# Local and global attention with a GELU feed-forward layer on one Trainium2 core: the fourth chunk's second layer in plain products, word checks from step 33, casts and penalties on ScalarE, row maxima put off, P6 first, outputs by SP

## The chip, the cores and the metric

The kernel runs on one core of a Trainium2 chip. The metric is device time in microseconds (us), the median of several executions. The engines go by their names in a profile: PE (TensorE's matrix products; PEld are its weight loads), DVE (VectorE), ACT (ScalarE), POOL (GpSimd) and SP (SyncE, which here only issues DMAs).

## The reference, cut to what matters

Attention over 4 batches, 8 heads, 768 positions and a head width of 64, with 8 global keys and a window of 96 local ones, and then a feed-forward layer on the 3072 rows of 512 that it gives:

```python
scores = scale * q @ k.T - slopes * dist        # kept where is_global | is_local, else -1e9
a = exp(scores - max(scores)); a = a / (sum(a) + 1e-09)
x = (a @ v).transpose(0, 2, 1, 3).reshape(B * S, H * D)   # 3072 x 512
h = x @ w_in                                              # 512 -> 2048
g = 0.5 * h * (1.0 + erf(h / sqrt(2)))
out = g @ w_out                                           # 2048 -> 512
```

The weights arrive as 64-bit floats and are read as pairs of 32-bit words.

## The kernel before, in words

**Chunks and steps.** The 3072 rows are cut into 12 chunks of 256 rows (c = 0 to 11), the 2048 hidden columns into 8 slices of 256 (s = 0 to 7). A step (c, s) computes one slice of both layers for one chunk. `STEPS` lists 99 places, T = 0 to 98: chunks 0 and 1 take turns up to T = 18, and from there chunk c owns the eight steps that begin at T = 19 + 8 (c - 2); so chunk 3 begins at T = 27, chunk 4 at 35, chunk 5 at 43. `run` walks over T and records, for each, the first layer of step T + 1 (`m1`, tile h), its GELU, the second layer of step T (`m2`), and pieces of the attention of a later chunk.

**Values as pairs.** Each factor is kept as two 16-bit halves, high and low, and a product is three products on PE (high by high, high by low, low by high). `m1` is 24 products of 256 columns. A plain `m2` (lines 853 to 868) is 12 products of 512 columns, into two PSUM banks `acc`. From chunk `SEVEN` = 3 on, `m2_seven` forms the second layer by Strassen's seven products P1 to P7: 21 products of 256 columns, into four banks `seven`. It needs sums of blocks on both sides: `gelu7` makes the left ones (tile ss, four DVE additions at line 742, then a cast `sh` on ACT and the low half `sl` on DVE) and `sums` the right ones, once for each slice (tiles sb, sf, sw; DVE, with one cast on ACT), at the steps that `SUMS` names.

**GELU.** ACT writes the value (gr). In the plain form DVE makes the high half (gh, line 834) and the low half (gl, line 204); in the form with sums ACT makes gh.

**Where the seven products live.** `HOME` gives each product a bank and a half of it: P1 and P2 share bank 0, P6 and P7 bank 1, P4 and P5 bank 2, and P3 has bank 3. At a chunk's last step `combine` empties them on DVE (tiles u and o, line 789) in the order bank 0, bank 1, bank 2, bank 3, while the next chunk's first step already computes. That step's products come in the order of `PARTS`: P1, P2, P4, then attention work of a later chunk, then P6, P7, P5, P3.

**Attention.** For a chunk from 3 on: score products (tile s), the subtraction of penalties with a running minimum on DVE (n, mn), exponentials on ACT, normalisation on POOL (line 554), a transposition on DVE (ptb), products with v (tile av; 256 small products and loads in a row), and the copies to x on ACT and DVE. The penalties come from `more_pens`; `scale_pens` multiplies them by each head's slope with eight POOL instructions at T = 14 and 15 (line 422).

**Checks.** Each of the 32 weight pieces is loaded a second time (tile c) and folded into a mask on DVE (`check_words`, tile wand), every second step from T = 21. `rows` takes row maxima of finished output (DVE, tile otop).

**What sets the order.** Within each engine a scheduler sorts the recorded instructions; `after`, `behind` and `turn` pin some of them. From T = 19 on PE's order is as recorded (`turn`). DMAs that one engine issues leave in its order; the outputs of the chunks with seven products are issued by ACT (line 823).

The two lines on which the order of products and the choice of form hang are:

```python
SEVEN = 3
PARTS = (("P1", "P2", "P4"), ("P6", "P7", "P5", "P3"))
```

Of the kernel before, what the change touches and what calls it, by code (L numbers as in the profile page):

```python
# [13 lines left out]
AF = mybir.ActivationFunctionType  # L14
ALU = mybir.AluOpType
# [3 lines left out]
P = 128  # L19
# [12 lines left out]
NCH = B * CPB  # L32
# [12 lines left out]
GAP = 3  # L45
# [12 lines left out]
CAT = 2  # L58
# [4 lines left out]
GS = 2.0 ** 6  # L63
# [1 line left out]
WMAX = 0.5  # L65
OMIN = 2.0 ** -10
RATIO = 16.0
SEVEN = 3
PARTS = (("P1", "P2", "P4"), ("P6", "P7", "P5", "P3"))
ENDS = (("P6", "P7", "P5"), (("P1", "P2", "P6", "P7"), ("P4", "P5", "P3")))  # L70
SUMS = {17: 0, 18: 1, 19: 2, 21: 3, 22: 4, 25: 5, 26: 6, 29: 7}
HOME = {"P1": (0, 0), "P2": (0, 1), "P6": (1, 0), "P7": (1, 1), "P4": (2, 0), "P5": (2, 1), "P3": (3, 0)}
FACTORS = {"P1": ("A11", "B11"), "P2": ("A12", "B21"), "P3": ("S4", "B22"), "P4": ("A22", "T4"), "P5": ("S1", "T1"),
           "P6": ("S2", "T2"), "P7": ("S3", "T3")}
# [2 lines left out]
NB = NW // NG  # L77
KA = NW + 2 * NG
PENS = 13


def dap(t, off, dims):
# [23 lines left out]
def slope(h):  # L106
    return 2.0 ** (-(h + 1))


class Fast:  # L110
# [225 lines left out]
            sync(vv[rows, :, 7, :], dap(self.v, b * S * DM + p * P, [[DM, NG], [2 * P, 2], [1, P]]))  # L336

    def load_v(self, c):
        if c >= SEVEN:
            return self.load_windows(c)  # L340
        self.vr[c] = self.nat.tile([P, 4, DM], F32, name=f"vr{c}", tag="vn")
        self.rows_v(self.sync_of(c, (3, 3)), self.vr[c], *divmod(c, CPB))

    def load(self, c):
        sync = self.sync_of(c, (3, 0))
        b, cc = divmod(c, CPB)
        k0 = b * H * D * S
        q0 = k0 + cc * CT
        every = [[S, P], [P * S, NP]]
        qr = self.nat.tile([P, NP, CT], F32, name=f"qr{c}", tag="qn")  # L350
        if c >= SEVEN:
            kr = self.nat.tile([P, NP, 2, 2 * KA], F32, name=f"kr{c}", tag="kn")
            sync(qr, dap(self.qT, q0, every + [[1, CT]]))
            for j in range(2):
                for a in range(2):
                    for o, n, k in self.runs(cc * CT + j * P + a * HQ - NC, NW):
                        sync(kr[:, :, j, a * KA + NG + o:a * KA + NG + o + n], dap(self.kT, k0 + k, every + [[1, n]]))
                    for o in (a * KA, a * KA + NG + NW):
                        sync(kr[:, :, j, o:o + NG], dap(self.kT, k0, every + [[1, NG]]))
            self.raw[c] = (kr, qr)  # L360
            return
        kr = self.nat.tile([P, NP, KW + 96 if cc == 0 else 2 * KW], F32, name=f"kr{c}", tag="kn",
                           padded_shape=[P, NP, 4 * KA])
        sync(qr, dap(self.qT, q0, every + [[1, CT]]))
        keys = lambda o, n, k: sync(kr[:, :, o:o + n], dap(self.kT, k, every + [[1, n]]))
        if cc == 0:
            keys(0, CT, k0)
            keys(CT, 96, k0)
            keys(CT + 96, NG, k0)
        else:  # L370
            keys(NG, NX + NC, q0 - 96)
            keys(224, NX, q0 + HQ)
            keys(KW, NX, q0 + 32)
            keys(KW + 96, NX + NC, q0 + 96)
            for o in (0, 192, KW + NX, KW + 256):
                keys(o, NG, k0)
        self.raw[c] = (kr, qr)
# [41 lines left out]
    def scale_pens(self, k):  # L419
        for i in range(4):  # L420
            h = 4 * (i // 2) + i % 2
            self.nc.gpsimd.tensor_scalar(out=self.pens2[k][:, i], in0=self.base[k], scalar1=8.0 * slope(h), scalar2=0.0,
                                         op0=ALU.mult, op1=ALU.add)

    def scores_windows(self, c, n):
        nc = self.nc
# [29 lines left out]
                self.last_dve = ins.ins  # L456

    def scores_pair(self, c, p):
        if c >= SEVEN:
            return self.scores_windows(c, p)  # L460

        nc = self.nc
# [63 lines left out]
    def exps(self, c, p):  # L526
        nc = self.nc
        first = c % CPB == 0
        mn, su = self.stat.pop((c, p))
        if c >= SEVEN:  # L530
            every = [(self.pt_n[c, p][:, i], i) for i in range(4)]
        else:
            every = [(self.pt_n[c, 2 * p + hh][:, j * NK:j * NK + (P if first and j == 0 else NK)], 2 * hh + j)
                     for hh in range(2) for j in range(2)]
        for nn, i in every:
            self.table(nc.scalar.activation(out=nn, in_=nn, func=AF.Exp, bias=mn[:, i:i + 1],  # L536
                                            scale=-1.0, accum_out=su[:, i:i + 1]))
        if c < SEVEN:
            self.norm(c, p, mn, su, every)
        else:  # L540
            self.normed[c, p] = mn, su, every

    def norm(self, c, p, mn, su, every):
        nc = self.nc
        ins = nc.vector.tensor_scalar(out=su, in0=su, scalar1=1e-9, scalar2=1.0 / XS, op0=ALU.add, op1=ALU.mult)
        if c >= SEVEN:
            self.behind(ins)
        nc.vector.reciprocal(out=su, in_=su)  # L548
        if c >= 3:
            top = self.nmax[:, 3 * NP]  # L550
            nc.vector.tensor_tensor(out=top, in0=top, in1=mn, op=ALU.max)
        for nn, i in every:
            eng = nc.vector if c < 2 else nc.gpsimd
            ins = eng.tensor_scalar(out=nn, in0=nn, scalar1=su[:, i:i + 1], scalar2=0.0,  # L554
                                    op0=ALU.mult, op1=ALU.add)
        if c < 2:
            self.last_dve = ins.ins
# [193 lines left out]
    def m2_seven(self, t, part):  # L751
# [2 lines left out]
            self.seven = [self.ps_acc.tile([P, 2, 256], F32, name=f"seven{i}", tag="ps_acc") for i in range(2)]  # L754
            self.seven += [self.bank([P, 2, 256], f"seven{i}") for i in range(2, 4)]
        back = len(STEPS) - 1 - t
        names = PARTS[part] if back > 1 or (back, part) == (1, 0) else ENDS[0] if back else ENDS[1][part]
        for name in names:
            if (back, name) == (0, "P3"):
                self.products(t - 1, name)  # L760
# [48 lines left out]
    def give(self, c, k, final):  # L809
# [10 lines left out]
        if c == NCH - 1:  # L820
            (nc.sync if k else nc.scalar).dma_start(self.out[r:r + P, 256:], o[:, 1])
            return
        nc.scalar.dma_start(self.out[r:r + P, :], o.rearrange("p h c -> p (h c)"))

    def gelu(self, t):
        nc = self.nc
# [4 lines left out]
        gl = self.gp.tile([P, 2, CT], F16, name=f"gl{t}", tag="gl")  # L831
        gr = self.gp.tile([P, 2, CT], F32, name=f"gr{t}", tag="gr")
        self.table(nc.scalar.activation(out=gr, in_=hp, func=AF.Gelu, scale=1.0 / (WS * XS)))
        nc.vector.tensor_scalar(out=gh, in0=gr, scalar1=GS, scalar2=None, op0=ALU.mult)
        self.last_dve = self.lo_dve(gl, gr, gh, GS).ins
        self.g[t] = (gh, gl)

    def m2(self, t, k):
# [12 lines left out]
                    self.send(k, kk)  # L851
            return
        if s == 0:
            if c == 1:
                self.acc[c, k] = self.bank([P, DM], f"acc{c}_{k}")
            else:
                self.acc[c, k] = self.ps_acc.tile([P, DM], F32, name=f"acc{c}_{k}", tag="ps_acc")
# [16 lines left out]
    def send(self, c, k):  # L874
# [3 lines left out]
        scale = 1.0 / (GS * WS)  # L878
        nc.scalar.activation(out=o, in_=acc, func=AF.Copy, scale=scale)
        nc.scalar.dma_start(self.out[r:r + P, :], o)  # L880
        self.rows(c, k, o)

    def rows(self, c, k, o):
        self.behind(self.nc.vector.tensor_reduce(out=self.otop[:, c, k], in_=o.rearrange("p (h c) -> p h c", h=2),
# [18 lines left out]
                         "av": self.av_pair}[what](c, p)  # L903

    def slot(self, at):
        for c in range(SEVEN, NCH):
            r = self.T - START[c]
            if 0 <= r < 8 and (r % 4, at) in SLOTS:
                what, n = SLOTS[r % 4, at]
# [13 lines left out]
    def run(self, flag_i):  # L923
# [15 lines left out]
        for self.T in range(START[0] - 1, last):  # L939
# [10 lines left out]
                    self.split_weights(s, i)  # L950
            if 0 <= T - last + 9 < 6:
                self.checks(T - last + 9)
            k = T - 16 - GAP
            if 0 <= k < 64 and k % 2 == 0:
                self.check_load(k // 2)
            words = 2 <= k < 66 and k % 2 == 0
            if words and (T < 30 or T % 4 == 1):
                self.check_words((k - 2) // 2)
            if T == PENS:
                self.more_pens()  # L960
            if PENS < T < PENS + 3:
# [30 lines left out]
            if T % 8 == 3:  # L992
                for args in self.late_rows:
                    self.rows(*args)
                self.late_rows.clear()
            if words and T >= 30 and T % 4 == 3:
                self.check_words((k - 2) // 2)

    def checks(self, k):
        nc, sm = self.nc, self.const  # L1000
# [221 lines left out]
```

## Time and profile before

| what | us |
|---|---|
| median of 3 runs | 631.32 |
| lowest and highest run | 628.44, 632.48 |
| the profiled execution's own time | 629.22 |
| its span, first to last instruction | 627.4 |
| PE busy in the span | 599.5 |
| DVE busy | 498.1 |
| ACT busy | 352.9 |
| POOL busy | 91.0 |

The profile shows one execution. Its times are counted from the first instruction; 1.8 us of the time lie around the span. A PE record's length is modelled and reaches over the start of the next product, so busy time says little there: a stretch is better read by the starts of successive products. TensorE's granted clock is full (2.4 GHz) in all the stretches named below.

### The profile page before, as it was taken

Reading aid. Unit: us, or ns where it says so; the run is one execution under the profiler, and the core shown is the slowest. Engines: PE = TensorE matmul, PEld = TensorE weight load, DVE = VectorE, ACT = ScalarE, POOL = GpSimd, SP = SyncE. Lnnn points to the kernel's source line nnn. Section 1 sums busy time; section 2 is a strip of 40 time slices with the busy share of each in tenths; the row PEclk is TensorE's granted clock in tenths of the full one; section 3 lists DMA queues with packets and bytes.
Section 4 is the critical chain, followed back from the end, with each engine's and each line's share of the span. In section 5 each row is a group of like instructions: output and inputs, shape, how many; then the busy total and the mean of one; then the engine's idle time right before and its main releaser. Section 6 shows DMA issues by size and latency. Waiting matters only on the chain.

```text
span 627.4 us, 19513 instructions
## 1 busy us (share of the span) xinstructions
PE 599.5 (96%) x7968; PEld 464.8 (74%) x7968; DVE 498.1 (79%) x1579; ACT 352.9 (56%) x855; POOL 91.0 (14%) x188
## 2 busy tenths in 40 slices
PE   8988999999999899999999899999999999999995
PEld 5665544445676678888888788888888888888884
DVE  7979999998788786876876776876876876875885
ACT  3777577755526566466466366366466466463331
POOL 1000006253033022022022021021021021010000
PEclk9988999999999999999999999999999999999998
DMA  9948925434371284184184175164275173100001
GB/s 272 270 173 255 261 97 202 121 66 146 114 192 57 86 218 137 37 218 136 37 218 137 36 186 159 46 159 129 104 169 180 44 195 93 37 1 2 36 1 40
DMA packets 111809, 79.47 MB, mean 127 GB/s; under 512 B 54752, under 2 KB 99296, under 8 KB 111712
## 3 DMA queue, kind: packets, MB, share of 16 engines
q1 hardware_dynamic: 107120, 70.80, 39.7%
q10 hardware_dynamic: 4592, 7.34, 3.3%
q8 instruction: 65, 1.06, 0.7%
q14 instruction: 32, 0.26, 0.1%
HBM read 71.83 MB, written 6.29 MB: 125 GB/s over the span
## 4 chain that ended last, share of the span: by engine, by line
PE 63%; DVE 23%; ACT 8%; issue 3%; POOL 2%; DMA 1%; DVEq 0%; ACTq 0%; POOLq 0%
PE h L702 26%; PE seven L776 22%; PE av L604 5%; ACT n L536 4%; PE s L440 4%; DVE gl L204 2%; DVE ss L742 2%; PE acc L863 2%; POOL n L554 2%; DVE wb L249 1%; DVE wb L251 1%; PE warm_ps L520 1%; DVE o L789 1%; DVE sl L204 1%; DVE u L789 1%
## 5 line engine op out<-in xcount | busy, mean ns | idle before, releaser
L702 PE MATMUL h<-x,winh 128*128 128x256 f16 x1344 | 227.7, 274 | 4.4 <-DVE x L203 2.9
L702 PE MATMUL h<-x,winl 128*128 128x256 f16 x672 | 184.3, 274 | 0.0
L702 PEld LDWEIGHTS <-winh 128*128 128x128 f16 x1344 | 130.3, 98 | 25.0 <-issue 4.0
L554 POOL TENSOR_SCALAR n<-n,su 128x160 f32<-128x160 f32 (+1 forms) x160 | 81.1, 527 | 450.0 <-DVE su L548 286.3
L737 ACT ACTIVATE gr<-h 128x512 f32<-128x512 f32 x72 | 43.0, 597 | 109.2 <-PE h L702 96.3
L742 DVE TENSOR_TENSOR ss<-gr 128x128 f32<-128x128 f32 x144 | 35.2, 285 | 64.6 <-ACT gr L737 64.6
L744 ACT ACTIVATE sh<-ss 128x512 f16<-128x512 f32 x72 | 45.4, 630 | 66.4 <-DVE ss L742 66.4
L776 PE MATMUL seven<-sw,sh 128*128 128x256 f16 x432 | 75.0, 273 | 1.3 <-issue 1.3
L702 PEld LDWEIGHTS <-winl 128*128 128x128 f16 x672 | 66.1, 98 | 9.1 <-issue 1.2
L776 PEld LDWEIGHTS <-sh 128*128 128x128 f16 x576 | 55.0, 98 | 8.3 <-issue 1.5
L536 ACT ACTIVATE n<-n,mn 128x160 f32<-128x160 f32 x144 | 59.5, 414 | 2.7 <-DVE mn L451 2.5
L776 PE MATMUL seven<-sw,sl 128*128 128x256 f16 x216 | 58.9, 273 | 1.2 <-DVE sl L204 1.1
L204 DVE SCALAR_TENSOR_TENSOR gl<-gr,gh 128x384 f16<-128x384 f32 (+1 forms) x96 | 57.1, 594 | 0.7
L204 DVE SCALAR_TENSOR_TENSOR sl<-ss,sh 128x512 f16<-128x512 f32 x72 | 49.6, 689 | 10.0 <-ACT sh L744 10.0
L776 PEld LDWEIGHTS <-gh 128*128 128x128 f16 x432 | 41.0, 98 | 11.9 <-ACT gr L737 3.8
L451 DVE CUSTOM_DVE_ANT_0 n<-s,pens 128x160 f32<-128x160 f32 x144 | 38.0, 320 | 3.8 <-PE s L440 2.5
L743 ACT ACTIVATE gh<-gr 128x384 f16<-128x384 f32 x72 | 37.6, 523 | 3.9 <-ACT gr L737 1.8
L776 PE MATMUL seven<-wouth,gh 128*128 128x256 f16 x144 | 39.4, 274 | 0.0
L776 PE MATMUL seven<-wouth,gl 128*128 128x256 f16 x144 | 39.3, 273 | 0.0
L776 PE MATMUL seven<-woutl,gh 128*128 128x256 f16 x144 | 39.3, 273 | 0.0
L604 PEld LDWEIGHTS av<-ptb,vr 32*64 32x64 f32 x2304 | 31.3, 130 | 5.6 <-issue 5.3
L536 ACT ACT_TABLE_LOAD x22 | 28.2, 1283 | 12.3 <-DMA qr<-qT 6.5
(160 smaller groups left out, 1103.5 us busy)
## 6 DMA issues: line engine op xcount, KB each, us to landing
w<-w SPq DMA_DIRECT2D x32, 512.0 KB, 6.4
c<-w SPq DMA_DIRECT2D x32, 512.0 KB, 4.5
kr<-kT SPq DMA_DIRECT2D x34, 320.0 KB, 4.2
vr<-v SPq DMA_DIRECT2D x60, 112.0 KB, 2.6
qr<-qT SPq DMA_DIRECT2D x11, 512.0 KB, 4.3
out<-o ACTq DMA_DIRECT2D x22, 256.0 KB, 2.3
kr<-kT SPq DMA_DIRECT2D x84, 64.0 KB, 3.6
vr<-v SPq DMA_DIRECT2D x36, 32.0 KB, 2.7
```

Of the source, the lines that this page charges most:

```text
L204: return self.nc.vector.scalar_tensor_tensor(out=out, in0=in_, scalar=scale, in1=hi, op0=ALU.mult, op1=ALU.subtract)
L440: ins = nc.tensor.matmul(sp[hh][NG * i:NG * i + NG, u, :], lhsT=qq[hr, 2 * e + p, o:o + NG], rhs=kt[hr, 2 * e + p, j, k:k + NW], start=Tru ...
L451: ins = nc.vector.tensor_tensor_reduce(out=nn[:, 2 * hh + u], in0=sp[hh][:, u, :], in1=pens, scale=-0.125, scalar=3e38, op0=ALU.add, op1=A ...
L536: self.table(nc.scalar.activation(out=nn, in_=nn, func=AF.Exp, bias=mn[:, i:i + 1], scale=-1.0, accum_out=su[:, i:i + 1]))
L554: ins = eng.tensor_scalar(out=nn, in0=nn, scalar1=su[:, i:i + 1], scalar2=0.0, op0=ALU.mult, op1=ALU.add)
L604: ins = nc.tensor.matmul(banks[i][hh * D:(hh + 1) * D, u0 * NG:u1 * NG], lhsT=vv[rows, e, b, hh * D:(hh + 1) * D], rhs=g, start=n == 0, st ...
L702: ins = nc.tensor.matmul(hp[:, f, :], lhsT=w[:, d, fs], rhs=x[:, d, e, :], start=n == 0, stop=n == 3 * NP - 1).ins
L737: self.table(nc.scalar.activation(out=gr.rearrange("p i q -> p (i q)"), in_=hp.rearrange("p f q -> p (f q)"), func=AF.Gelu, scale=1.0 / (W ...
L742: self.last_sum = nc.vector.tensor_tensor(out=ss[:, o], in0=x, in1=y, op=op).ins
L743: nc.scalar.activation(out=gh, in_=gr[:, 1:], func=AF.Copy, scale=GS)
L744: self.last_table = nc.scalar.activation(out=sh, in_=ss, func=AF.Copy, scale=GS).ins
L776: ins = nc.tensor.matmul(out, lhsT=g, rhs=w, start=s == 0 and name in ("P1", "P4", "P6", "P3") and i == 0, stop=s >= NST - 4 and i == 2, s ...
```

## The change

Seven edits, none of which alters what is computed.

1. `SEVEN` goes from 3 to 4: chunk 3's second layer is done in plain products. Its attention keeps the form with windows, which now hangs on a constant of its own, `TURNS` = 3. The right-hand sums are made later (`SUMS`), and chunk 3's two `acc` banks come from the shared pool of banks.
2. The word checks (load, DVE instruction) move from steps 21 to 83 to steps 33 to 89.
3. In plain steps from chunk 2 on, ACT makes gh in place of DVE.
4. `scale_pens` moves from POOL to ACT.
5. The row maxima of the plain chunks after the first are put off to the next step with T % 8 == 3.
6. In a chunk's first step P6 comes third and P4 fifth (`OPENS`).
7. Outputs of the chunks with seven products are issued by SP in place of ACT.

```diff
-SEVEN = 3
+SEVEN = 4
+TURNS = 3
 PARTS = (("P1", "P2", "P4"), ("P6", "P7", "P5", "P3"))
+OPENS = (("P1", "P2", "P6"), ("P7", "P4", "P5", "P3"))
-SUMS = {17: 0, 18: 1, 19: 2, 21: 3, 22: 4, 25: 5, 26: 6, 29: 7}
+SUMS = {18: 0, 21: 1, 22: 2, 25: 3, 26: 4, 27: 5, 29: 6, 30: 7}
+WORDS = [T for T in range(33, 90) if T % 2 or T in (62, 70, 78)]
...
-            self.nc.gpsimd.tensor_scalar(out=self.pens2[k][:, i], in0=self.base[k], scalar1=8.0 * slope(h), scalar2=0.0,
-                                         op0=ALU.mult, op1=ALU.add)
+            self.nc.scalar.activation(out=self.pens2[k][:, i], in_=self.base[k], func=AF.Copy, scale=8.0 * slope(h))
...
-        names = PARTS[part] if back > 1 or (back, part) == (1, 0) else ENDS[0] if back else ENDS[1][part]
+        names = OPENS[part] if s == 0 else PARTS[part] if back > 1 or (back, part) == (1, 0) else ENDS[0] if back else ENDS[1][part]
...
-        nc.scalar.dma_start(self.out[r:r + P, :], o.rearrange("p h c -> p (h c)"))
+        nc.sync.dma_start(self.out[r:r + P, :], o.rearrange("p h c -> p (h c)"))
...
-        nc.vector.tensor_scalar(out=gh, in0=gr, scalar1=GS, scalar2=None, op0=ALU.mult)
+        if STEPS[t][0] < CAT:
+            nc.vector.tensor_scalar(out=gh, in0=gr, scalar1=GS, scalar2=None, op0=ALU.mult)
+        else:
+            self.last_table = nc.scalar.activation(out=gh, in_=gr, func=AF.Copy, scale=GS).ins
...
-            if c == 1:
+            if c % 2:
                 self.acc[c, k] = self.bank([P, DM], f"acc{c}_{k}")
...
-        self.rows(c, k, o)
+        if c:
+            self.late_rows.append((c, k, o))
+        else:
+            self.rows(c, k, o)
...
-            k = T - 16 - GAP
-            if 0 <= k < 64 and k % 2 == 0:
-                self.check_load(k // 2)
-            words = 2 <= k < 66 and k % 2 == 0
-            if words and (T < 30 or T % 4 == 1):
-                self.check_words((k - 2) // 2)
+            if T + 2 in WORDS:
+                self.check_load(WORDS.index(T + 2))
+            if T in WORDS and T % 4 == 1:
+                self.check_words(WORDS.index(T))
...
-            if words and T >= 30 and T % 4 == 3:
-                self.check_words((k - 2) // 2)
+            if T in WORDS and T % 4 > 1:
+                self.check_words(WORDS.index(T))
```

**DVE, between the low half of GELU 28 and the copies to x of chunk 4's first half.** A number in a name is its step or chunk: gl28 is the low half of step 28, av4 the products with v of chunk 4. Before:

```order
L204 SCALAR_TENSOR_TENSOR sl27_2688<-ss27_2686,sh27_2687 128x512
L884 TENSOR_REDUCE otop_141<-o2_0_2704 128x2
L884 TENSOR_REDUCE otop_141<-o2_1_2714 128x2
L278 SCALAR_TENSOR_TENSOR wand_135<-c0_3_2578,wand_135 128x512
L203 TENSOR_TENSOR sw6_1246<-sf6_2649,sw6_1246 128x1024
L742 TENSOR_TENSOR ss28_2749<-gr28_2746 128x128 x2
L742 TENSOR_TENSOR ss28_2749<-ss28_2749,gr28_2746 128x128
L742 TENSOR_TENSOR ss28_2749<-gr28_2746,ss28_2749 128x128
L204 SCALAR_TENSOR_TENSOR gl28_2748<-gr28_2746,gh28_2747 128x384
L204 SCALAR_TENSOR_TENSOR sl28_2751<-ss28_2749,sh28_2750 128x512
L203 TENSOR_TENSOR x_346<-av4_0_0_2774,x_346 128x128
```

Now (line numbers are those of the changed kernel, 2 to 8 higher):

```order
L207 SCALAR_TENSOR_TENSOR gl27_2655<-gr27_2656,gh27_2654 128x512
L724 TENSOR_TENSOR sb5_2678<-wouth5_1093,woutl5_1094 128x1024
L727 TENSOR_TENSOR sf4_2620<-sb4_2619,sf4_2620 128x256
L727 TENSOR_TENSOR sf5_2679<-sb5_2678 128x256 x2
L727 TENSOR_TENSOR sf5_2679<-sb5_2678,sf5_2679 128x256
L206 TENSOR_TENSOR sw4_989<-sf4_2620,sw4_989 128x1024
L727 TENSOR_TENSOR sf5_2679<-sb5_2678,sf5_2679 128x256
L207 SCALAR_TENSOR_TENSOR gl28_2713<-gr28_2714,gh28_2712 128x512
L206 TENSOR_TENSOR sw5_1095<-sf5_2679,sw5_1095 128x1024
L206 TENSOR_TENSOR x_346<-av4_0_0_2725,x_346 128x128
```

The left-hand sums of step 28, two row maxima and a word check are gone from ahead of x; the right-hand sums of another slice have come in before gl28.

**PE, the first step of chunk 5 (T = 43), from P2 to the products with v.** Before, with P4 (bank `seven2`) third:

```order
L776 MATMUL seven0_2761<-wouth0_327,gl43_4384 128x256
L776 LDWEIGHTS gh43_4383
L776 MATMUL seven2_2763<-sw0_329,gh43_4383 128x256
L776 LDWEIGHTS gl43_4384
L776 MATMUL seven2_2763<-sw0_329,gl43_4384 128x256
L604 MATMUL av6_0_0_4482<-ptb6_0_4354,vr6_4276 64x128 x2
```

Now, with P6 (bank `seven1`) there:

```order
L778 MATMUL seven0_3447<-wouth0_327,gl43_4217 128x256
L778 LDWEIGHTS sh43_4219
L778 MATMUL seven1_3448<-sw0_329,sh43_4219 128x256
L778 LDWEIGHTS sl43_4220
L778 MATMUL seven1_3448<-sw0_329,sl43_4220 128x256
L606 MATMUL av6_0_0_4315<-ptb6_0_4187,vr6_4109 64x128 x2
```

The third product now writes bank 1 and reads the left-hand sums sh and sl in place of gh and gl; P4 stands behind the products with v and P7.

**ACT, around the GELU of step 17.** Before:

```order
L833 ACTIVATE gr16_1670<-h16_1649 128x512
L581 COPY pt2_4_1660<-t2_5_1674 128x384
L833 ACTIVATE gr17_1714<-h17_1693 128x512
L581 COPY pt2_6_1704<-t2_6_1700 128x384
L581 COPY pt2_6_1704<-t2_7_1718 128x384
```

Now:

```order
L835 ACTIVATE gr16_1670<-h16_1649 128x512
L583 COPY pt2_4_1660<-t2_5_1674 128x384
L425 ACTIVATE pens_132<-rb_1453 128x640 x4
L425 ACTIVATE pens2_1451<-rb_1453 128x320 x4
L835 ACTIVATE gr17_1714<-h17_1693 128x512
L583 COPY pt2_6_1704<-t2_6_1700 128x384
L583 COPY pt2_6_1704<-t2_7_1718 128x384
```

The eight scalings of the penalties (pens, from tile rb) now stand ahead of gr17 and of two copies that empty PSUM banks.

## Rows read from the trace of the kernel before

**Rows 1.** Page, busy time: engine, us, share of the span, instructions.
```profile
PE 599.5 (96%) x7968; PEld 464.8 (74%) x7968; DVE 498.1 (79%) x1579; ACT 352.9 (56%) x855; POOL 91.0 (14%) x188
```

**Rows 2.** Page, the chain that ended last, shares by engine.
```profile
PE 63%; DVE 23%; ACT 8%; issue 3%; POOL 2%; DMA 1%; DVEq 0%; ACTq 0%; POOLq 0%
```

**Rows 3.** Chain in order of time: start us, us, what; from two plateaus.
```profile
176.02 2.59 PE acc L863 x12
...
570.92 2.29 PE seven L776 x21
```

**Rows 4.** Waits of PE, 140 to 260 us: us in total, times, longest us.
```profile
PE h L702 <- DVE x L203: 2.7, 2, 2.3
PE s L440 <- DVE x L203: 1.3, 1, 1.3
PE seven L776 <- DVE sl L204: 1.1, 1, 1.1
PE acc L863 <- DVE gh L834: 0.8, 1, 0.8
PE seven L776 <- DVE u L789: 0.4, 1, 0.4
PE acc L863 <- DVE gl L204: 0.2, 1, 0.2
```

**Rows 5.** Timeline of PE around 210 us: start us, us, instruction, [idle before <-releaser].
```profile
209.50 0.27 PE L776 MATMUL seven<-wouth,sl 128*128 128x256 f16 x1
212.06 0.38 PE L702 MATMUL h<-x,winh 128*128 128x256 f16 x2 [2.29 <-DVE x L203]
```

**Rows 6.** Timeline of DVE in the same stretch.
```profile
207.66 0.68 DVE L278 SCALAR_TENSOR_TENSOR wand<-c,wand 128x512 int32<-128x512 int32 x1
...
211.72 0.88 DVE L203 TENSOR_TENSOR x<-av,x 128x128 f16<-128x128 f32 x4
```

**Rows 7.** Waits of PE, whole span.
```profile
PE seven L776 <- DVE u L789: 2.5, 7, 0.4
...
PE seven L776 <- issue: 1.8, 2, 1.3
```

**Rows 8.** Timeline of PE where chunk 4 begins.
```profile
256.18 0.27 PE L776 MATMUL seven<-wouth,gl 128*128 128x256 f16 x1
256.81 0.38 PE L776 MATMUL seven<-sw,gh 128*128 128x256 f16 x2 [0.36 <-DVE u L789]
```

**Rows 9.** Timeline of DVE in the same stretch.
```profile
254.74 0.42 DVE L789 SCALAR_TENSOR_TENSOR u<-seven,u 128x256 f32<-128x256 f32 x1
255.08 0.69 DVE L204 SCALAR_TENSOR_TENSOR sl<-ss,sh 128x512 f16<-128x512 f32 x1
...
256.34 0.42 DVE L789 SCALAR_TENSOR_TENSOR u<-seven,u 128x256 f32<-128x256 f32 x1
```

**Rows 10.** Page, costliest groups: busy us, mean ns of one.
```profile
L742 DVE TENSOR_TENSOR ss<-gr 128x128 f32<-128x128 f32 x144 | 35.2, 285 | 64.6 <-ACT gr L737 64.6
L744 ACT ACTIVATE sh<-ss 128x512 f16<-128x512 f32 x72 | 45.4, 630 | 66.4 <-DVE ss L742 66.4
...
L204 DVE SCALAR_TENSOR_TENSOR sl<-ss,sh 128x512 f16<-128x512 f32 x72 | 49.6, 689 | 10.0 <-ACT sh L744 10.0
...
L743 ACT ACTIVATE gh<-gr 128x384 f16<-128x384 f32 x72 | 37.6, 523 | 3.9 <-ACT gr L737 1.8
```

**Rows 11.** Groups by line, same columns.
```profile
L727 ACT CAST sw<-sf 128x1024 f16<-128x1024 f32 x8 | 8.4, 1045 | 17.5 <-DVE sf L725 17.5
```

**Rows 12.** Timeline of ACT at step 16.
```profile
131.47 0.60 ACT L833 ACTIVATE gr<-h 128x512 f32<-128x512 f32 x1 [2.70 <-DVE gl L204]
```

**Rows 13.** Timeline of DVE at step 16.
```profile
131.39 0.66 DVE L416 TENSOR_SCALAR rb<-rb 64x960 f32<-64x960 f32 x1
```

**Rows 14.** Timeline of PE at step 16.
```profile
133.90 0.39 PE L848 MATMUL acc<-wouth,gh 128*128 128x512 f16 x1
```

**Rows 15.** Page, DMA queues: packets, MB, share of 16 engines.
```profile
q8 instruction: 65, 1.06, 0.7%
```

More of the change, by code (lines that the diff above doesn't have):

```diff
@@ L338, in load_v @@
     def load_v(self, c):
-        if c >= SEVEN:
+        if c >= TURNS:
             return self.load_windows(c)
@@ L350, in load @@
         qr = self.nat.tile([P, NP, CT], F32, name=f"qr{c}", tag="qn")
-        if c >= SEVEN:
+        if c >= TURNS:
             kr = self.nat.tile([P, NP, 2, 2 * KA], F32, name=f"kr{c}", tag="kn")
@@ L458, in scores_pair @@
     def scores_pair(self, c, p):
-        if c >= SEVEN:
+        if c >= TURNS:
             return self.scores_windows(c, p)
@@ L529, in exps @@
         mn, su = self.stat.pop((c, p))
-        if c >= SEVEN:
+        if c >= TURNS:
             every = [(self.pt_n[c, p][:, i], i) for i in range(4)]
@@ L537, in exps @@
                                             scale=-1.0, accum_out=su[:, i:i + 1]))
-        if c < SEVEN:
+        if c < TURNS:
             self.norm(c, p, mn, su, every)
@@ L545, in norm @@
         ins = nc.vector.tensor_scalar(out=su, in0=su, scalar1=1e-9, scalar2=1.0 / XS, op0=ALU.add, op1=ALU.mult)
-        if c >= SEVEN:
+        if c >= TURNS:
             self.behind(ins)
@@ L905, in slot @@
     def slot(self, at):
-        for c in range(SEVEN, NCH):
+        for c in range(TURNS, NCH):
             r = self.T - START[c]
```

## The prediction

> **What bounds the kernel now.** I read the page first. PE is busy for 96% of the span [rows 1] and carries 63% of the chain that ended last, DVE 23% [rows 2]: the reader is to see that the end is mostly PE's own work, so that two things count, the products issued and the places where PE stands still. The chain in order of time gives the price of work in stretches without a gap: a plain step's second layer takes 2.59 us (12 products of 512 columns, 0.216 each), one by seven products 2.29 us (21 of 256 columns, 0.109 each) [rows 3]. Last came PE's waits, then the timelines around the long ones. Between 140 and 260 us, chunks 2 and 3 above all, PE is let go by DVE each time [rows 4]: DVE makes the right-hand sums of all eight slices there, beside word checks and row maxima, and x comes late. From there on a wait of 0.36 us comes back where a new chunk begins, seven times with 2.5 us in all [rows 7].
>
> An idle time understates what a wait costs. The product before a gap is recorded with 0.27 us, but its successor could start after 0.11; so the gap ahead of 212.06, after a product begun at 209.50, costs 212.06 - 209.50 - 0.11 = 2.45 us where the row says 2.29 [rows 5]. I add 0.16 us to each wait.
>
> **The change part by part.**
>
> *Chunk 3 in plain products* adds on PE 8 steps x (2.59 - 2.29) = +2.4 us [rows 3], on the path, for PE has no slack there. It takes from DVE, for each of these steps, four sums of 0.285 us and one low half of 0.689 [rows 10]: 1.8 us, 14.6 us in all (the other low half grows from 384 to 512 columns, which I leave out). On its two acc banks: chunk 4 needs them some 3.6 us into its first step (24 x 0.109 of first layer, three products of 0.33), and ACT empties them in two copies, by the row for 512 columns about 0.63 each [rows 10]; no wait.
>
> *Word checks, later sums, row maxima, gh to ACT.* In the order shown, DVE loses ahead of chunk 4's first x the sums of step 28, two row maxima and a check, and gains one slice's right-hand sums, of which most stand before gl28. Before, wand began at 207.66 and x only at 211.72 [rows 6], while PE wanted it at 209.61. Seven checks leave the steps up to 33, and chunk 2's eight gh instructions leave DVE; on ACT one such cast of 512 columns takes about 0.63 us [rows 10], behind gr and ahead of gl, and ACT is busy for only 56% [rows 1]. So I let the waits of 140 to 230 us go: 2.7 + 1.3 + 1.1 + 0.8 + 0.2 = 6.1 us of idle [rows 4] (the 0.4 on u is left to the edit after this), plus six times 0.16, makes 7.1. I keep 0.3 of it, since the first right-hand sum still stands ahead of gl at the beginning of chunk 2: -6.8 us. What is late next is the sums at steps 29 and 30, in chunk 3; they have no left-hand sums beside them any more. From step 33 the checks come at the rate at which they came before (one in two steps, three more), where DVE shows no wait but the one on u.
>
> *P6 first.* At 256.18 the second product ends its issue; P4 starts at 256.81 [rows 8], because its bank is free only after DVE's third u (256.34 + 0.42). Bank 1, which P6 needs, is free after the u that begins at 254.74, and sl, P6's last factor, is written from 255.08 to 255.77 [rows 9]; P6 would start at 256.29 and want sl 0.22 later. P4 moves behind the products with v and P7. All seven waits go (six by this, that of chunk 4 by the plain chunk ahead of it): 2.5 + 7 x 0.16 = 3.6 us [rows 7]: -3.6 us.
>
> *Penalties on ACT* is the edit that can cost. The trace shows no such instruction on ACT. The nearest rows are a cast of 384 columns with 0.523 and of 512 with 0.630 us [rows 10]; a straight line gives 0.74 for 640 and 0.47 for 320 columns, for four of each 4.8 us. Bounds: four at no less than 0.63 and four at half of that, 3.8; four at the 1024-column cast's 1.045 [rows 11] and four at 0.63, 6.7. They wait for tile rb, written by 131.39 + 0.66 = 132.05 [rows 13]; gr17, which began at 131.47 [rows 12], then begins at 136.9 (135.9 to 138.8) and ends 0.6 later. Behind it wait two copies that empty banks, and on those banks PE's next scores; PE comes to them after the 12 products from 133.90 [rows 14], 133.90 + 12 x 0.216 = 136.5. So PE stands for 1.0 us (0 to 2.9). Instructions in a row overlap a little; I take +0.6. POOL loses as much work.
>
> The Trainium skill (ScalarE: Activation LUTs, What ACT_TABLE_LOAD costs) puts an ACTIVATE with immediate scale and bias at 186 ns plus 0.833 ns a column, with an overlap of 93 ns in a row; an estimate by it is 3.9 us for the eight, and PE's wait would be 0.1 us. The row for 512 columns agrees (613 ns by the rule, 630 measured).
>
> *Outputs by SP* takes from ACT a wait for DVE's last u and o. It held gr only where PE had other work, so I count nothing. On SP the two DMAs wait at most for the four microseconds in which DVE empties the banks; behind them stand the loads of a chunk that is used three steps (over 15 us) later. Cover gone: nothing up to that lead.
>
> *Sum* against the profiled execution of 629.22 us (span 627.4 and 1.8 around it): +2.4 - 6.8 - 3.6 + 0.6 = -7.4, so 621.8 us. The median of the runs, 631.32, is 2.1 above that execution; I carry the same difference over: 631.3 - 7.4 = 623.9, or 624.0 us.
>
> **The rivals.**
>
> 1. *The waits come back in another place.* The right-hand sums are as much work as before, now packed between T = 18 and 30, and x of chunk 4 still stands behind a sum's last instruction. If half of the 6.8 returns: 627.4 us. For it: the order above has sw5 directly ahead of x. Against it: DVE is rid there of 14.6 us of left-hand sums and of seven checks of 0.68 [rows 6].
> 2. *P6 first does not do what it says.* If sl or sh is late where DVE is full, P6 waits as P4 did, and 3.1 of the 3.6 us stay (six starts): 627.1. For it: sl ends only 0.7 us before it is wanted.
> 3. *Penalties dear.* With the upper bound PE stands 2.9 us in place of 0.6: 626.3.
> 4. *Instruction supply, to the slower side.* Two of PE's waits in the second product, 1.8 us, have no releaser but "issue" [rows 7], right behind the 256 dense instructions of the products with v. Queue 8 loads instructions, 65 packets of 1.06 MB [rows 15], that is 16 KB for some 245 of PE's 15,936, if all are PE's. The change takes 144 instructions from PE ahead of chunk 4, so the ends of these pieces fall elsewhere in each later pass. Seven chunks' attention, 14 passes, lies behind that place. If each stalled by the longest of these waits (1.3 + 0.16 = 1.5 us), that adds 21 us less the 2.1 that now stand: 643. It decides from about six passes on (7.4 us eaten) and is slower by over 1% from about eleven. Against it: the pieces fall at all places over the passes as it is, and two or three stall.
> 5. *No such stall at all*: the two waits vanish with the new places, 624.0 - 2.1 = 621.9.
>
> The Trainium skill (Runtime: NRT & Kernel Launch, Instruction fetch mechanics) has the sequencer load 256 instructions at a time beside execution and calls a boundary's cost mostly hidden. By it case 5 would hold in every run; the trace differs, with 1.3 us in one wait.
>
> **How the numbers follow.** The forecast has 0.47, rival 1 0.20, rival 2 0.10, rival 3 0.07, rival 4 0.08 and rival 5 0.08. About 1% of 631.3, 6.3 us, is what a measurement of this kernel can tell from no change (its three runs lie 4.0 us apart): faster means below 625.0. The forecast is only 1.0 us beyond it, so I give 0.37 of its 0.47 to faster; with rival 5 and some of rivals 1 and 3 (0.07) that makes 0.52. Slower comes from rival 4's upper part alone, 0.05 and some for what I haven't seen, 0.07. The same keeps 0.41. The range goes down to 619.0 (rival 5, with the lower bound of the penalties and 2 us of scatter) and up to 631.0 (rivals 1 and 2 together, 630.5).
>
> **What would show it.** Right: no wait of PE on x, gh or sl between 140 and 230 us; none on u at a chunk's start; chunk 3's second layer at 2.59 us a step; a wait of under 1 us on the banks at step 17; everything ahead of 130 us as before. Wrong: PE waiting for ACT at step 17 for over 2 us; waits on x or gl at steps 29 to 32; P6 waiting for sl; more "issue" waits behind the products with v.

## The result and the profile after

The changed kernel takes 621.57 us in the median of 4 runs (620.33 to 624.53), the kernel before 629.88 beside it; the ratio is 0.987 with an interval of 0.983 to 0.992. The median had been forecast at 624.0, from 631.3 for the kernel before, which came out 1.4 lower this time; the difference, 8.3 us against 7.4, is the fairer measure. The profiled execution takes 621.09 us with a span of 619.3, 8.1 us less than that of before. Page, busy time of the changed kernel and the chain that ended last:

```profile
PE 599.3 (97%) x7896; PEld 457.8 (74%) x7896; DVE 479.8 (77%) x1523; ACT 358.6 (58%) x865; POOL 81.4 (13%) x180
PE 77%; DVE 12%; ACT 4%; DMA 2%; issue 2%; SPq 2%; POOL 1%; ACTq 0%; DVEq 0%; POOLq 0%
```

Against [rows 1, 2]: PE has 72 products fewer and the same busy time, DVE's share of the chain has halved. The waits of PE from 125 us on (us in total, times, longest us):

```profile
PE acc L868 <- ACT gh L839: 1.0, 1, 1.0
PE h L704 <- DVE x L206: 0.9, 1, 0.9
PE av L606 <- issue: 0.7, 1, 0.7
PE seven L778 <- issue: 0.4, 1, 0.4
```

Of [rows 4] one wait on x and one on gh are left, the one on gh now for ACT; the seven on u of [rows 7] are gone, and "issue" has shrunk from 2.8 us in three waits (one of them on av) to 1.1 in two. Where chunk 5 begins, PE's timeline has no idle time between P2, P6 and the products with v, where [rows 8] showed P4 waiting at chunk 4's start:

```profile
300.34 0.27 PE L778 MATMUL seven<-wouth,gl 128*128 128x256 f16 x1
300.45 0.38 PE L778 MATMUL seven<-sw,sh 128*128 128x256 f16 x2
300.67 0.27 PE L778 MATMUL seven<-sw,sl 128*128 128x256 f16 x1
300.87 1.80 PE L606 MATMUL av<-ptb,vr 32*64 32x128 f32 x128
```

The starts of the same products set side by side give the account of the 8.1 us: up to step 17's first layer 0.7 later; chunk 3 in plain products +2.4 (0.30 in each of eight steps); the waits up to 230 us -5.2 (what is left of that stretch when the other terms are taken off); the seven waits on u -3.8; the waits for issue -1.8; the rest -0.4. What is left at T = 28 is seen on DVE, where x stands behind the low half of the sum recorded at T = 27:

```profile
207.93 1.23 DVE L206 TENSOR_TENSOR sw<-sf,sw 128x1024 f16<-128x1024 f32 x1 [0.51 <-ACT sw L729]
209.07 0.88 DVE L206 TENSOR_TENSOR x<-av,x 128x128 f16<-128x128 f32 x4
```

Ahead of step 19's second layer it is on ACT: the cast of the first sum stands before gr19, which had its h at about 152, and gh19 comes behind both:

```profile
152.72 1.05 ACT L729 CAST sw<-sf 128x1024 f16<-128x1024 f32 x1 [2.77 <-DVE sf L727]
...
153.67 0.59 ACT L835 ACTIVATE gr<-h 128x512 f32<-128x512 f32 x1
154.29 0.63 ACT L839 ACTIVATE gh<-gr 128x512 f16<-128x512 f32 x1
```

### The profile page after: what moved, and what is told of

It is laid out like the page before. It is cut to its first block, busy times and chain, and to the rows that moved or that the text cites. A ratio compares the mean times of both kernels' runs of the same rounds, so it can differ in the third digit from the quotient of the medians.

```text
span 619.3 us, 19315 instructions
## 1 busy us (share of the span) xinstructions
PE 599.3 (97%) x7896; PEld 457.8 (74%) x7896; DVE 479.8 (77%) x1523; ACT 358.6 (58%) x865; POOL 81.4 (13%) x180
## 4 chain that ended last, share of the span: by engine, by line
PE 77%; DVE 12%; ACT 4%; DMA 2%; issue 2%; SPq 2%; POOL 1%; ACTq 0%; DVEq 0%; POOLq 0%
PE h L704 33%; PE seven L778 23%; PE acc L868 6%; PE av L606 5%; PE s L442 4%; PE h L698 3%; PE acc L853 2%; SPq L318 2%; DVE wb L252 1%; DVE wb L254 1%; DMA kr<-kT 1%; ACT n L538 1%; DVE gl L207 1%; DVE wb L249 1%; POOL n L556 1%
## 5 line engine op out<-in xcount | busy, mean ns | idle before, releaser
L739 ACT ACTIVATE gr<-h 128x512 f32<-128x512 f32 x64 | 38.2, 597 | 94.6 <-PE h L704 92.5
L746 ACT ACTIVATE sh<-ss 128x512 f16<-128x512 f32 x64 | 40.3, 630 | 61.7 <-DVE ss L744 61.7
L778 PE MATMUL seven<-sw,sh 128*128 128x256 f16 x384 | 67.4, 273 | 0.0
L778 PEld LDWEIGHTS <-sh 128*128 128x128 f16 x512 | 48.9, 98 | 6.6 <-issue 0.6
L778 PE MATMUL seven<-sw,sl 128*128 128x256 f16 x192 | 52.3, 273 | 0.5 <-issue 0.4
L207 DVE SCALAR_TENSOR_TENSOR sl<-ss,sh 128x512 f16<-128x512 f32 x64 | 44.2, 691 | 9.4 <-ACT sh L746 9.4
L778 PEld LDWEIGHTS <-gh 128*128 128x128 f16 x384 | 36.5, 98 | 7.3 <-ACT gr L739 3.3
L778 PE MATMUL seven<-wouth,gh 128*128 128x256 f16 x128 | 35.0, 274 | 0.0
L778 PE MATMUL seven<-wouth,gl 128*128 128x256 f16 x128 | 34.9, 273 | 0.0
L778 PE MATMUL seven<-woutl,gh 128*128 128x256 f16 x128 | 34.9, 273 | 0.0
```

Source lines behind the costliest of these rows:

```text
L207: return self.nc.vector.scalar_tensor_tensor(out=out, in0=in_, scalar=scale, in1=hi, op0=ALU.mult, op1=ALU.subtract)
L739: self.table(nc.scalar.activation(out=gr.rearrange("p i q -> p (i q)"), in_=hp.rearrange("p f q -> p (f q)"), func=AF.Gelu, scale=1.0 / (W ...
L746: self.last_table = nc.scalar.activation(out=sh, in_=ss, func=AF.Copy, scale=GS).ins
L778: ins = nc.tensor.matmul(out, lhsT=g, rhs=w, start=s == 0 and name in ("P1", "P4", "P6", "P3") and i == 0, stop=s >= NST - 4 and i == 2, s ...
```

## The experiments

Twelve runs followed. The start scatters: step 17's first layer began 2.0 us earlier to 0.6 later than in the changed kernel's profile (144 more left out), though hardly anything differs ahead of it. The granted clock goes along with it: the earliest trace (seven products from chunk 3, 126.2 us) has no stretch recorded at the lower level (1.2 GHz) ahead of that step, six have one and begin step 17 at 127.1 to 127.7, six have two and begin it at 127.6 to 128.8. Whole runs show the same: the 38 runs of the kernel before go from 627.0 us with a mean granted clock of 0.997 to 635.0 with 0.984.

So the runs are compared by stretches, from the start of one product to that of another in both traces: I from the first layer of step 17 to that of step 37, II from there to that of step 76, III from there to the end of the span. The stretches are those of the one profiled execution, and in P4 third, outputs by ACT, seven products from chunk 3 and sums spread that was the longest of its runs. Stretch I is within 0.1 us in the five traces whose edits lie behind or ahead of it (changed kernel again, P4 third, outputs by ACT, both of these, 144 more), so 0.3 us can be told there; III holds the end behind PE's last product too, which alone differs by -0.6 to +0.8. Differences from the changed kernel, in us:

| run | median (lowest to highest) | I | II | III |
|---|---|---|---|---|
| kernel before | 631.04 (626.98 to 634.99) | +3.4 | +5.6 | -0.2 |
| changed kernel again | 620.24 (619.21 to 623.31) | +0.1 | 0.0 | -0.2 |
| P4 third | 624.65 (623.91 to 627.15) | 0.0 | +1.7 | +5.5 |
| outputs by ACT | 623.99 (622.61 to 625.28) | 0.0 | +2.5 | +1.1 |
| both of these | 627.98 (624.75 to 629.68) | +0.1 | +2.5 | +4.1 |
| seven products from chunk 3 | 621.37 (620.23 to 623.10) | +1.1 | +5.1 | -2.1 |
| penalties on POOL | 619.74 (618.43 to 621.36) | -0.3 | 0.0 | 0.0 |
| word checks from 21 | 623.47 (622.80 to 626.14) | +1.5 | +1.2 | -0.1 |
| gh on DVE | 621.27 (620.64 to 622.47) | +0.9 | 0.0 | -0.9 |
| row maxima at once | 621.98 (621.47 to 624.82) | +1.6 | +0.1 | +0.1 |
| sums spread | 622.90 (621.19 to 624.03) | +2.4 | 0.0 | +0.2 |
| sums from 20 | 621.45 (619.82 to 623.25) | -0.3 | +0.2 | -1.3 |
| 144 more | 635.36 (634.11 to 637.12) | 0.0 | +3.8 | -1.1 |

**P4 third.**

```diff
-OPENS = (("P1", "P2", "P6"), ("P7", "P4", "P5", "P3"))
+OPENS = PARTS
```

> The changed kernel with P4 third again in a chunk's first step. Theory A (the forecast's step): the wait of P4 for DVE's u comes back at the six chunk starts T = 43 to 83, not at T = 35, where no seven products lie ahead, 0.36 us of idle or 0.53 of start-to-start time each: 3.2 us more, about 624.8 us. Theory B (rival 2: the place of P6 does nothing, and the waits are gone for another reason, such as outputs by SP): no such waits, 621.6 us.

Six waits on u came back, as theory A has it, 0.4 us of idle each, four of them in II (1.7 us). The median lies 3.1 above 621.57. But the profiled execution, 627.15, is the longest of its four (the others, 623.9 to 625.1, lie where theory A puts them), and its stretch III grew by 5.5, of which the two u make 0.9. The timeline of PE at T = 75, and then the windows around it:

```profile
486.80 0.38 PE L778 MATMUL seven<-sw,gh 128*128 128x256 f16 x2 [0.36 <-DVE u L791]
487.01 0.27 PE L778 MATMUL seven<-sw,gl 128*128 128x256 f16 x1
487.21 1.84 PE L606 MATMUL av<-ptb,vr 32*64 32x128 f32 x125
490.74 0.30 PE L606 MATMUL av<-ptb,vr 32*64 32x32 f32 x3 [1.68 <-issue]
```

```profile
core 0: us, PE busy (x) PEld busy (x) DVE busy (x) ACT busy (x) POOL busy (x), PEclk, DMA share, GB/s
480.00:488.00 8.00, 7.64 (x116) 6.60 (x118) 7.63 (x22) 3.24 (x6) 0.00 (x0) 1.00 0.08 32
492.00:495.50 3.50, 3.50 (x20) 2.53 (x18) 1.45 (x3) 0.00 (x0) 0.00 (x0) 0.52 0.24 60
496.00:500.00 4.00, 4.00 (x76) 3.06 (x82) 2.56 (x14) 2.53 (x4) 0.00 (x0) 1.00 0.07 27
```

Behind a wait of 0.36 and one of 1.68 us within some four microseconds, the granted clock stood at 0.52 from 492.0 to 495.5, the lower of its two levels (1.2 GHz), and the products came at half their pace: some 1.7 us more (3.5 x 0.48). The waits for issue, three in place of two, make up the rest.

**Outputs by ACT.** `nc.sync.dma_start` in `give` is `nc.scalar.dma_start` again.

> The changed kernel with the outputs of the chunks with seven products issued by ACT again. Theory A (the forecast's step: it held ACT's gelu by some 1.8 us at a chunk's start, where PE had other work): 621.6 us within 0.3. Theory B (with P6 third, sh and sl of the first step are wanted earlier, so that the hold shows on PE): six or seven waits on sl or gh at the chunk starts T = 43 to 91, 0.2 to 0.5 us each: 2 to 3 us more, about 624 us.

Theory B in its sum, in another place: six waits, but of the products with v, whose bank gr must read out first. ACT's timeline where chunk 5 begins, and PE's wait:

```profile
301.21 0.34 ACTq L825 DMA_DIRECT2D out<-o  x1
301.60 0.60 ACT L739 ACTIVATE gr<-h 128x512 f32<-128x512 f32 x1 [1.82 <-DVE u L791]
```

```profile
302.25 1.04 PE L606 MATMUL av<-ptb,vr 32*64 32x128 f32 x55 [0.33 <-ACT gr L739]
```

The first output's DMA waits on ACT for DVE's u and o, and gr behind it. Start to start it is 0.6 us each time (once 0.9).

**Both of these.**

> The changed kernel with both undone: P4 third in a chunk's first step and outputs issued by ACT. Alone, the one cost six waits for DVE's u (0.52 us of start-to-start time each), the other six waits of the products with v for ACT's gr (0.58 each, one 0.87). Theory A: the two waits lie one behind the other in the same half microsecond, and either edit alone gains next to nothing: together six waits of 0.5 to 0.6 us, 2.6 to 3.3 us more than the changed kernel, not 5.5; about 624.5 us. Theory B: they add up: about 627 us.

Theory A by the waits: six on u (2.4 us of idle), none on gr; stretch II has the same 2.5 us as outputs by ACT alone. The median of 628.0, which looks like theory B, has its rest in stretch III, as far as the profile shows: a wait for issue of 1.6 us at T = 75, the lower clock behind it, and one of 0.7 behind the pass of T = 83. The profiled execution, 626.74 at a mean granted clock of 0.992, lies 1.2 below the median; the twelve runs go from 624.75 at 0.996 to 629.68 at 0.989, and where those above the profiled one lose their time no trace shows. So by the waits the two edits do not add up; by the medians (3.1 and 2.4 alone, 6.4 together) they do, and more.

**Seven products from chunk 3**, with the sums at the steps of before.

> The changed kernel with seven products from chunk 3 on again and the right-hand sums at the steps of before; the other edits stay. Theory A (the plain chunk is paid back by a DVE that is rid of 14.6 us of left-hand sums): 2.4 us fewer products, but the waits on x at T = 28 and on sl come back with 3 to 4 us in all, and the 144 PE instructions move the issue waits back to the places of before, 1.8 more: about 624.5 us. Theory B (the waits came from checks, row maxima and gh, which are out of the way; the plain chunk is a pure cost): no such waits, 2.4 less and 1.8 more, about 621.0 us.

Between the theories. In stretch I it is 1.1 us slower although its products take 2.4 less, so waits of some 3.4 us came back: at T = 18 1.2 for gr and 0.8 for x, at T = 27 and 30 1.3 for sh and sl (idle); the one on x at T = 28 did not. The run changes the form of chunk 3 and the places of the sums together, so it does not show which of the two brought back those at T = 18. Stretch II has two of the waits for issue at the places of before (T = 47 and 51, 0.9 and 2.0 us) and the lower clock behind the second. The medians, 621.37 against 621.57, show no difference.

**Penalties on POOL.**

> The changed kernel with the penalties scaled on POOL again. Theory A (PE shows no wait on a bank at T = 17 in the changed kernel, so ACT's eight instructions cost nothing and POOL's would cost nothing either): 621.6 us within 0.3. Theory B (the forecast's +0.6: ACT's work is paid somewhere): 621.0 us. Theory C (POOL beside DVE makes DVE's instructions longer, as xtop showed before with 1.20 in place of 0.68 us, and holds PE around 137 and 149 us): 0.5 to 1.0 us more, about 622.3 us.

Nearest to theory A: -0.3 us in stretch I, nothing in the others; the 619.74 lies within the scatter of the starts. But the 0.3 is a difference of two things. From step 17's first layer to step 19's, POOL's version is 0.25 us slower; behind it, it is 0.55 faster, since the wait on gh at T = 19 is 0.3 us of idle in place of 1.0. Theory C's mechanism is there too, though PE hardly pays for it: while POOL scales (131.98 to 138.58), DVE's maximum over x takes 1.20 us, and 0.69 with the scalings on ACT; two more of its instructions grow as much. POOL's version and then the changed kernel:

```profile
133.39 1.20 DVE L211 TENSOR_TENSOR xtop<-x 128x1024 f16<-128x1024 f16 x1
```

```profile
133.91 0.69 DVE L211 TENSOR_TENSOR xtop<-x 128x1024 f16<-128x1024 f16 x1
```

In the changed kernel ACT's eight scalings took 4.05 us and gr17 began at 136.73, with the two copies behind it:

```profile
132.77 4.05 ACT L425 ACTIVATE pens<-rb 128x640 bf16<-128x640 f32 x8 [3.30 <-DVE rb L419]
136.73 0.58 ACT L835 ACTIVATE gr<-h 128x512 f32<-128x512 f32 x1
137.21 0.84 ACT L583 COPY pt<-t 128x384 f32<-128x384 f32 x2
```

PE's scores began at 137.36, 0.05 us behind gr17's end, and their second half at 138.10, 0.05 behind that of the copies. The products ahead of them had begun at 136.98 and 137.94, so PE stood some 0.2 us there, which its idle rows do not list.

**Word checks from 21; gh on DVE; row maxima at once.** Each undoes one edit.

> The changed kernel with the word checks at the steps of before, T = 21 to 83. Seven checks of 0.68 us come back on DVE between T = 21 and 33, one of them (T = 27) near the x that PE waits for at T = 28. Theory A (DVE is full there): the wait of 1.1 us at T = 28 grows by the length of one check, 0.7 us, and others of up to 1 us in all come up at T = 21 to 32: 0.7 to 1.7 us more, about 622.7 us. Theory B (the plain chunk alone has freed DVE, the checks find room): 621.6 us.

> The changed kernel with gh of chunks 2 and 3 on DVE again (16 casts of 0.43 us, 6.9 us). Theory A (DVE is full up to T = 34): the waits at T = 20 and T = 28, now 1.5 and 1.1 us, grow by 0.4 to 0.9 us each: 1 to 2 us more, about 623.1 us. Theory B (ACT's gh is itself what PE waits for at T = 20, by 1.2 us, so DVE's shorter cast is better there): up to 0.6 us less, about 621.0 us.

> The changed kernel with the row maxima of the plain chunks made at once (chunks 1 to 3, two of 0.67 us each). Theory A: they stand ahead of x or gl at T = 19, 27 and 35 on a full DVE: the wait of 1.1 us at T = 28 grows by up to 0.7, that at T = 20 by up to 0.7: 0.5 to 1.4 us more, about 622.5 us. Theory B: DVE is waiting for others at these places (it stood 1.1 us idle for ACT's sw at T = 19 and 0.5 at T = 28), so they cost nothing: 621.6 us.

In stretch I all three lie near theory A: +1.5, +0.9 and +1.6 us; the medians, 1.9 above to 0.3 below 621.57, do not tell the last two from the changed kernel. With the row maxima the wait on x at T = 28 went from 0.9 to 2.5 us of idle; with gh on DVE that on gh from 1.0 to 1.5 and that on x from 0.9 to 1.3. The checks moved their waits: the one on x was gone, and others of 0.5 and 0.9 us (and 0.3 on gl) stood at T = 29 and T = 31. The 1.2 and -0.9 us in the other stretches are waits for issue.

**Sums spread; sums from 20.** Two tries at the waits that are left; both have the word checks from T = 37.

```diff
-SUMS = {18: 0, 21: 1, 22: 2, 25: 3, 26: 4, 27: 5, 29: 6, 30: 7}
+SUMS = {21: 0, 22: 1, 25: 2, 26: 3, 29: 4, 30: 5, 33: 6, 34: 7}
```

> The changed kernel with the right-hand sums at T = 21, 22, 25, 26, 29, 30, 33, 34, the steps in which no x is made, and the word checks from T = 37. Theory A: what is left of PE's waits in chunks 2 and 3 hangs on the sums' places: at T = 20, 1.2 us for gh, since ACT's cast of the first sum stands ahead of gr19, and 0.3 for gl; at T = 28, 1.1 us for x, since x stands behind the low half of the sum of T = 27. Both go: 2.5 us less from T = 17 on, about 619.1 us. Theory B: DVE has no room at T = 33 to 35 beside the first left-hand sums, and PE waits there for sl or sh of step 35, which P6 wants third: 1 to 2 us of it come back, about 620.5 us.

> As the one before, but the sums at T = 20, 21, 22, 25, 26, 29, 30, 33, so that none stands at T = 34. Theory A: no wait at T = 20 and 28, and none at T = 35: 2.5 us less from T = 17 on, about 619.1 us. Theory B: three sums in a row at T = 20 to 22 hold gl or x up to T = 24: a wait of 0.5 to 1.5 us there, about 620 us.

In both, the waits on gh (it stands at T = 19, not at T = 20 as the text above has it) and on x at T = 28 are gone, which shows what they hung on. Sums spread has theory B's two waits at T = 35 (0.5 each for sh and sl). Neither theory had the third thing. PE's waits from 125 us on, for sums spread and then for sums from 20:

```profile
PE av L606 <- issue: 1.6, 1, 1.6
PE av L606 <- DMA vr<-v: 1.2, 1, 1.2
PE seven L778 <- ACT sh L746: 0.5, 1, 0.5
PE seven L778 <- DVE sl L207: 0.5, 1, 0.5
```

```profile
PE av L606 <- DMA vr<-v: 1.2, 2, 0.8
```

PE, no longer held ahead of step 19's second layer, now waits within it, in the products with v, for the load of chunk 3's v, which SP issues in 16 DMAs over some 10 us. The wait on gh had covered it. So in sums from 20, 2.5 us removed brought 0.3. In sums spread the clock came on top: behind the wait for v the products of step 19's second layer came at half their pace.

```profile
159.00:161.00 2.00, 2.00 (x46) 0.90 (x34) 1.34 (x5) 0.77 (x4) 0.00 (x0) 0.57 0.03 8
161.00:162.00 1.00, 1.00 (x4) 0.38 (x3) 0.73 (x2) 0.00 (x0) 0.00 (x0) 0.50 0.00 0
```

That is 1.2 us in six products (2.54 from the first to the layer behind them, 1.31 in sums from 20) and a little more behind, the larger part of the +2.4 in stretch I. No version beats the changed kernel by more than the scatter.

**144 more.** In `warm`, 24 products of 512 columns are cut in four of 128.

> The changed kernel with 144 more PE instructions at the very start (24 of the 512-column warm-up products are cut in four of 128 columns each, so 72 more loads and 72 more products for the same columns). In both traces PE has waits without a releaser: before 1.2, 1.5 and 0.6 us at or just behind the products with v of T = 47, 51 and 55; after the change 0.9 and 0.6 us at T = 75 and 79. Counted in PE's own order of instructions, each of the five products that come late has a number that leaves the same rest by 256 (192 or 193). Theory A, instruction supply in pieces of 256: with 144 more ahead, chunk 4 and all later ones stand at the places of the kernel before, so the three waits come back at T = 47, 51 and 55 with 1.2, 1.5 and 0.6 us and those at T = 75 and 79 are gone: 3.3 us in place of 1.5, so 1.8 us more than the changed kernel, about 623.4 us. Theory B, the waits belong to the time or to other traffic: they stay at T = 75 and 79 or go to other places, and the time stays at 621.6 us.

The cut was not free. These products came at 0.21 us each, and the first uncut ones behind them, at 25.7 to 27.5 us, at 0.43, so a cut one took twice as long as a whole one. Nor was that the full pace: 512 columns take 0.23 from 31 us on. In the changed kernel that change, from 0.43 to 0.23, comes at about 7 us. The clock column reads 1.00 in all these places, so it is the pace that tells the lower level here. The first products of 144 more, and then those of the changed kernel:

```profile
1.47 10.50 PE L525 MATMUL warm_ps<-wz 128*128 128x128 f32 x48 [1.47 <-DVE nmax L174]
```

```profile
1.46 5.45 PE L522 MATMUL warm_ps<-wz 128*128 128x512 f32 x12 [1.46 <-DVE nmax L174]
7.26 1.20 PE L522 MATMUL warm_ps<-wz 128*128 128x512 f32 x4
```

So the start became 12.7 us longer, and the median says nothing here. The places say it. The pass at T = 47 in the kernel before, and with 144 more:

```profile
327.33 1.74 PE L604 MATMUL av<-ptb,vr 32*64 32x128 f32 x120
330.03 0.32 PE L604 MATMUL av<-ptb,vr 32*64 32x32 f32 x8 [0.95 <-issue]
```

```profile
336.75 1.68 PE L609 MATMUL av<-ptb,vr 32*64 32x128 f32 x119
339.92 0.32 PE L609 MATMUL av<-ptb,vr 32*64 32x32 f32 x9 [1.49 <-issue]
```

The waits at T = 47, 51 and 55 came back (1.7, 0.9 and 0.8 us start to start), with one more of 0.5 behind the pass of T = 63, and those at T = 75 and 79 went. Counted in PE's order (loads, products and the sequencer's own instructions), the late product has the numbers 7616, 8385 and 9152 before, and 7616, 8385, 9152 and 10688 here. In all 14 traces together 24 such waits of over 0.4 us beyond the usual pitch were found, and every number leaves 192 or 193 by 256. Theory A holds for the places.

**The changed kernel again.**

> The changed kernel itself, once more, as the measure for the other runs of this call. If PE's waits without a releaser are a matter of the place in PE's instructions, they stand again at T = 75 and T = 79, with 0.5 to 1.3 us each, whatever the start of the run does; the time is 621.6 us within 1.5. If they come by chance of traffic, they stand at other steps.

The wait at T = 75 stood again at number 12737 (1.2 us of idle); the one at T = 79 stood at its place too, with 0.1 in place of 0.4. So the place is fixed and the length is not. Over the runs with number 12737 in this pass (12736 where P4 is third), it goes with the time at which the 16 KB on the instruction queue begin to come: 1.9 us ahead of the pass no wait, 0.1 us behind its start 0.9, 0.6 behind 1.4, 1.2 behind 1.9; two runs stand out: sums spread, where the transfer itself took 1.7 us in place of 0.9 to 1.1, and outputs by ACT, whose pass had just waited for gr (0.4 behind, 0.6 of wait). What sets that start stays open; it was latest in the two kernels in which P4 had just waited.

## Why the prediction was right, point by point

**What bounds the kernel** was read rightly: behind the start, the end moved by PE's own work and PE's stand-stills, and in some runs by the lower clock behind one of these. The 0.7 us that the start took are not explained; both profiles have two stretches at the lower clock there.

**Chunk 3 in plain products**: +2.4 forecast, +2.4 measured. What it pays back is small: with seven products there and the sums at their old places, some 3.4 us of waits return, so the edit is worth 1.1 us in stretch I, and nothing in the medians.

**The waits of 140 to 230 us**: -6.8 forecast, -5.2 measured. The step that failed is "I keep 0.3 of it, since the first right-hand sum still stands ahead of gl". What stayed is 2.5 us start to start, only 0.3 of it on gl: gh behind ACT's cast of that sum, and x behind the sum of T = 27, which is rival 1's mechanism in about a third of its size. The text had named "sw5 directly ahead of x" and then let it go. The stretch shrank by some 0.6 us more than its listed waits did; that part is not traced to single waits.

**P6 first**: -3.6 forecast, -3.8 measured; but the reason given is half of it. **Outputs by SP**: "It held gr only where PE had other work, so I count nothing" is wrong. PE had other work only as long as P4 waited for u. Either edit alone leaves a wait of half a microsecond at each start; the 3.8 us belong to the pair, as far as these waits go.

**Penalties**: +0.6 forecast; some 0.2 at the banks and 0.3 in all by the run with POOL. The path was read rightly, for PE's scores were let go by gr17 and by the copies; the term that was mis-sized is the scalings, 4.8 us against 4.05 (the prediction's other estimate, 3.9, takes off eight overlaps where eight instructions in a row have seven, and comes to 4.0). That gr17 began 0.2 us from its forecast (136.9 against 136.73) is luck: the start made all of it 0.7 later. A cost that the forecast did not have lies further on: by the same run, 0.7 us of the wait on gh at T = 19.

**Rivals 4 and 5.** The waits for issue were counted unchanged; they fell by 1.8 us, nearly all of rival 5's gain, by the way the pieces of 256 happen to fall. Rival 4's mechanism is the right one (pieces that end in or behind a dense pass) but its size was not: at most four waits stood in any run, never fourteen, as the ends of the pieces fall at another place of each pass. The Trainium skill (Runtime: NRT & Kernel Launch, Instruction fetch mechanics) gives blocks of 256 instructions; the 24 waits agree. It calls the cost of a boundary mostly hidden; behind 256 instructions issued in 1.8 us it was up to 2.0 us here.

The forecast of -7.4 against -8.1 in the profile is thus better than its parts, and that is luck: 1.6 us too much on the waits were made up by 1.8 for issue, which the forecast counted as unchanged; the 0.6 for the penalties, which PE hardly paid, and 0.6 of small terms gained more than was forecast, and the start took back 0.7. Two of the signs named for a right forecast did not come: PE still waits on gh and on x between 140 and 230 us, and what lies ahead of 130 us was not as before.

## What to carry to other kernels

Two waits may stand one behind the other in the same half microsecond: before an edit is credited with a wait, look for what the next instruction would have waited for, and undo the edits one at a time and together. Where the start of a run scatters by more than an edit is worth, compare from one product to another behind it. And of waits without a releaser, count the place in the engine's own instructions before explaining them by traffic.

## What the runs showed of the hardware that was not expected

- Waits for issue on PE stood at one rest (192 or 193) by 256 of PE's instruction number in 13 of 14 traces, 24 times, with 0.4 to 2.0 us beyond the usual pitch.
- A wait on u and one for issue close together (0.36 and 1.68 us of idle) were followed by 3.5 us of granted clock at 0.52, which cost some 1.7 us: as much as the wait itself. Two such waits did the same in the run with both edits undone (0.35 and 1.65), and so did one for issue of 2.0 us alone (seven products from chunk 3) and one for v of 1.2 us at the beginning of a pass (sums spread, 0.57 from 159 to 161 us); one of 1.5 (144 more) and one of 1.6 (sums spread, T = 75) did not, nor did 0.36 and 1.34 in the kernel before.
- Ahead of 30 us in 144 more, a product of the 32-bit type with 128 columns took half as long as one with 512 (0.21 and 0.43 us), so cutting it in four doubled its time.
- While POOL ran its scalings, one and the same DVE instruction over 128x1024 values took 1.20 us (two traces); with these on ACT it took 0.68 to 0.69 (twelve traces).
